# FFN weight combinations stored once in fp32 and split where they are used

## The chip, the cores and the metric

The kernel runs on one core of a Trainium2 chip. The metric is the device time of one execution in microseconds, as the median of several runs. The kernel before the change: 3426.71 us, median of 3 runs (3424.28 to 3429.13).

## What is computed

One transformer block for 2048 rows of width 576, with a modulation from a condition vector, 32 query heads over 16 key heads, a window of the last 512 keys, and a gated FFN of width 4608. Everything is float32.

```python
mod = (silu(c) @ w_mod).reshape(c.shape[0], 6, 1, -1)
sa, ca, ga, sb, cb, gb = (mod[:, i] for i in range(6))
h = layernorm(x) * (1 + ca) + sa
q = (h @ wq), 32 heads of 128
k, v = k_cache[:, :, -512:], v_cache[:, :, -512:], each for two query heads
p = softmax(q @ k.T * 128 ** -0.5)
x = x + ga * ((p @ v) @ wo)
h = layernorm(x) * (1 + cb) + sb
x = x + gb * ((sigmoid(h @ w_gate) * (h @ w_up)) @ w_down)
```

## The kernel before

**Arithmetic.** A float32 value is split into `hi`, its rounding to the type fp32r (a ScalarE copy with F32R as target), and `lo`, the rest (one subtraction). A product is three matmuls: hi x lo, lo x hi, hi x hi (`three`, line 272). Where weights are multiplied, the kernel uses a scheme with seven block products in place of eight: for w_gate/w_up, for w_down and for wo, sums and differences of blocks ("combinations") are formed first.

**Stage 1, attention** (loop at line 912). 128 blocks (a head and 512 queries), four steps each, so 512 steps `n`. A step does the scores of step n+2 (`scores`, `expo`), transposes the probabilities of step n (`transp`), does a quarter of the next-but-one query projection (`qproj`) and a quarter of the product with v of the block before (`pv`). ScalarE makes the exponentials `pp`, the hi copies `ptt` and `qt`; DVE the row maxima `neg`, the lo parts, and the scaled result `ov`. The reciprocal sums of a block go to DRAM and come back broadcast to all partitions (`put_rs`, `get_rs`, tile `rb`); `put_o` stores `ov` per block to `oscr`.

Beside the steps run **background jobs** (lines 675 to 831), listed by step in `at_step`. They read w_gate, w_up and w_down, form the combinations, split them in hi and lo, and store both to DRAM (`wsc`, `dsc`). There are 135 jobs, one each 3 steps: two per column tile of w_gate/w_up ("ab", one for each 128 rows), one per four tiles for the last 32 rows ("tail"), three per pair of row tiles of w_down ("down"). A job loads at step n, sums on GpSimd at n+3, makes hi on ScalarE at n+6 and lo on GpSimd at n+7, stores at n+8 and n+9. Its rooms lie in the tiles x0 and x1, whose contents are parked elsewhere by then, and in `extra`: three rooms for raw pieces, and two for `hi` (`(k % 2) * 7 * P` in line 708). 48 jobs for wo, one each 9 steps, form wo's combinations in tiles of their own and store them unsplit to `wosc`. All these instructions are pinned in program order with those around them (`pin`, `keep_order`); instructions that are not pinned may be moved by the scheduler.

**Stage 2, the product with wo** (line 1218). 32 visits (8 heads, 512 rows in four tiles) of seven products of 12 matmuls. `w_load` fetches a combination of wo, `w_split` splits it (ScalarE, and GpSimd or DVE), `v_load`, `v_sum` and `v_split` do the same for attention's result (tiles `vr`, `vt`, `vh`). DVE adds the products to x. In the last visits come the layer norm and the block sums for the FFN.

**Stage 3, the FFN** (line 1250). 72 rounds `u`: two pairs of row blocks by 36 column tiles. A round has seven products of seven matmuls of 512 columns (`product`, line 1112) with weights `sw`, loaded from `wsc` nine ahead (`load_w`), hi and lo in one DMA. Between them stand 42 matmuls of 288 columns with w_down (`down`, tile `sd`, `load_sd`, seven ahead), whose results DVE adds to the accumulators in x (`x<-w,x`; four banks `w`). ScalarE takes sums out of PSUM (`keep`), does sigmoids and hi copies (`hl`), GpSimd the lo parts and sums (`hl`, `vs`). Between the two pairs the input combinations are transposed anew (`load_combo`) and the results put together (`finish`).

In the profile nearly all rows are at L36, the helper that records instructions; tiles tell them apart. `x` is the background's rooms in stage 1, the residual in stage 2, the accumulators in stage 3.

Of the kernel before, what the change touches and what calls it, by code (L numbers as in the profile page):

```python
# [16 lines left out]
P = 128  # L17
# [27 lines left out]
def adaln_block_kernel(ctx: ExitStack, tc: tile.TileContext, x, k_cache, v_cache, wq, wo, w_gate, w_up, w_down,  # L45
# [251 lines left out]
    extra = at.tile([P, 4 * P], F32, tag="extra", name="extra")  # L297
# [187 lines left out]
    def expo(n):  # L485
        b, i = divmod(n, TPB)
        PP[n] = at.tile([P, W], F32, tag="pp", name="pp", bufs=2)
# [22 lines left out]
    def pv(b, k):  # L510
# [7 lines left out]
        if k == KT - 1:  # L518
            o = at.tile([P, BLK], F32, tag="ov", name="ov", bufs=2)
            by_tile = RB.pop(b).rearrange("p (q i) -> p i q", i=TPB)  # L520
            nc.vector.tensor_mul(o.rearrange("p (i q) -> p i q", i=TPB),
                                 OP_[b].rearrange("p (i q) -> p i q", i=TPB), by_tile)
            OT[b] = o
            del OP_[b], PT[b]
# [12 lines left out]
    def put_o(b):  # L537
        half, hd, blk = blk_of(b)
        to = oscr[half][hd // 8][:, :, 2 * (blk % 2) + hd % 2, hd // 2 % 4, :]
        keep_order(nc.sync.dma_start(to, OT.pop(b).rearrange("p (i q) -> p i q", i=TPB)))  # L540
# [138 lines left out]
    DW = D2 // 3  # L679
    jobs = []  # L680
    for f in range(NF):
        jobs += [("ab", f, 0), ("ab", f, 1)]
        if f % 4 == 3:
            jobs.append(("tail", f - 3, 0))
    jobs += [("down", g, s) for g in range(NF // 2) for s in range(3)]
# [14 lines left out]
    def bg_load(k, b0):  # L700
        kind, f, s = jobs[k]
        w = DW if kind == "down" else P
        raw = bg_view(b0, (k % 3) * 4 * P, [4, w])
        if k % 3 == 2:
            sums = extra[:, : 4 * w].rearrange("p (a b) -> p a b", a=4)
        else:
            sums = bg_view(b0 + 1, 14 * P, [4, w]) if k % 3 else bg_view(b0, 12 * P, [4, w])
        hi = bg_view(b0 + 1, (k % 2) * 7 * P, [8 if kind == "down" else 7, w])
        BG[k] = [raw, sums, hi]
        if kind == "down":  # L710
            for half, (i, j) in enumerate(((0, 1), (3, 2))):
                n0 = half * D2 + s * DW
                for c, slot in enumerate((i, j)):
                    r0 = (2 * f + c) * P
                    pin(nc.sync.dma_start(raw[:, slot, :], w_down[r0 : r0 + P, n0 : n0 + DW]))
            return
        if kind == "ab":
            r0, cc = s * P, slice(f * P, (f + 1) * P)
            g = w_gate[:, cc].rearrange("(c r) n -> r c n", c=2)[r0 : r0 + P]
            pin(nc.sync.dma_start(raw[:, 0:2, :], g))  # L720
            pin(nc.sync.dma_start(raw[:, 3, :], w_up[r0 : r0 + P, cc]))
            pin(nc.sync.dma_start(raw[:, 2, :], w_up[D2 + r0 : D2 + r0 + P, cc]))
            return
        for slot, w, r0 in ((0, w_gate, 2 * P), (1, w_gate, D2 + 2 * P), (3, w_up, 2 * P), (2, w_up, D2 + 2 * P)):
            src = w[r0 : r0 + TQ, f * P : (f + 4) * P].rearrange("r (q n) -> q r n", q=4)
            pin(nc.sync.dma_start(raw[:, slot, :], src))

    def bg_sums(k):
        r, m, hi = BG[k]
        kind, f, s = jobs[k]  # L730
        x0, x1, x2, x3 = [r[:, i, :] for i in range(4)]
        if kind == "down":
            for half in range(2):
                n0 = half * D2 + s * DW
                v = r[:, 2 * half : 2 * half + 2, :]
                g = rows2["gate"][:, None, n0 : n0 + DW].to_broadcast([P, 2, DW])
                pin(nc.gpsimd.tensor_mul(v, v, g))
            t1, t2, t3, t4 = [m[:, i, :] for i in range(4)]
            pin(nc.gpsimd.tensor_sub(t1, x3, x0))
            pin(nc.gpsimd.tensor_sub(t2, x2, t1))  # L740
            pin(nc.gpsimd.tensor_sub(t3, x2, x3))
            pin(nc.gpsimd.tensor_sub(t4, x1, t2))
            return
        s1, s2, s4, s3 = [m[:, i, :] for i in range(4)]
        pin(nc.gpsimd.tensor_add(s1, x3, x2))
        pin(nc.gpsimd.tensor_sub(s2, s1, x0))
        pin(nc.gpsimd.tensor_sub(s3, x0, x3))
        pin(nc.gpsimd.tensor_sub(s4, x1, s2))


    def bg_pairs(k):
        r, m, hi = BG[k]
        plain = [(7, 8, r[:, 3:4, :])] if jobs[k][0] == "down" and jobs[k][1] == NF // 2 - 1 else []
        return [(0, 3, r[:, 0:3, :]), (3, 7, m)] + plain

    def bg_hi(k):
        hi = BG[k][2]
        for a, b, v in bg_pairs(k):
            pin(nc.scalar.activation(hi[:, a:b, :].bitcast(F32R), v, AF.Copy))

    def bg_lo(k):
        hi = BG[k][2]
        for a, b, v in bg_pairs(k):
            pin(nc.gpsimd.tensor_sub(v.bitcast(F32R), v, hi[:, a:b, :]))

    def bg_store(k, part):
        kind, f, s = jobs[k]
        if part and kind != "tail":
            return
        hi = BG[k][2]  # L770
        if kind == "tail":
            for q in (0, 1) if part == 0 else (2, 3):
                rows = slice(q * TQ, (q + 1) * TQ)
                for to in range(4):
                    for a, b, src in bg_pairs(k) if to % 2 else [(0, 7, hi)]:
                        pin(nc.sync.dma_start(wsc[f + q][to * TQ : (to + 1) * TQ, a:b, 4, :], src[rows]))
        else:
            if kind == "down":
                to = [dsc[f][:, :, i, s * DW : (s + 1) * DW] for i in range(2)]
            else:  # L780
                to = [wsc[f][:, :, 2 * s + i, :] for i in range(2)]
            n = bg_pairs(k)[-1][1]
            pin(nc.sync.dma_start(to[0][:, :n], hi[:, :n]))
            for a, b, lo in bg_pairs(k):
                pin(nc.sync.dma_start(to[1][:, a:b, :], lo))
        if part or kind != "tail":
            del BG[k]

    STEP = 3
    slots = list(range(9, N - 50, STEP))[: len(jobs)]  # L790
    assert len(slots) == len(jobs)
# [8 lines left out]
    WOJ = {}  # L800

    def wo_load(k):
        g, c = divmod(k, 3)
        t = wp.tile([P, 7, DW], F32, tag="woj", name="woj", bufs=2)
        WOJ[k] = t
        for half, (i, j) in enumerate(((0, 1), (5, 2))):
            n0 = half * D2 + c * DW
            for h, slot in enumerate((i, j)):
                r0 = (2 * g + h) * P
                pin(nc.sync.dma_start(t[:, slot, :], wo[r0 : r0 + P, n0 : n0 + DW]))  # L810

    def wo_sums(k):
        t, c = WOJ[k], k % 3
        lo, hi = [rows2["gate1"][:, n0 : n0 + DW] for n0 in (c * DW, D2 + c * DW)]
        pin(nc.gpsimd.tensor_mul(t[:, 0:2, :], t[:, 0:2, :], lo[:, None, :].to_broadcast([P, 2, DW])))
        for slot in (2, 5):
            pin(nc.gpsimd.tensor_mul(t[:, slot, :], t[:, slot, :], hi))
        b11, b21, b22, t1, t2, b12, t4 = [t[:, i, :] for i in range(7)]
        pin(nc.gpsimd.tensor_sub(t1, b12, b11))
        pin(nc.gpsimd.tensor_sub(t2, b22, t1))  # L820
        pin(nc.gpsimd.tensor_sub(b12, b22, b12))
        pin(nc.gpsimd.tensor_sub(t4, b21, t2))

    def wo_store(k):
        g, c = divmod(k, 3)
        pin(nc.sync.dma_start(wosc[g // 4][:, :, g % 4, c * DW : (c + 1) * DW], WOJ.pop(k)))

    for k in range(3 * (H // 2)):
        at_n(32 + 9 * k, wo_load, k)
# [571 lines left out]
```

## Time and profile before

| | |
|---|---|
| median of the runs | 3426.71 us |
| the profiled execution | 3420.56 us |
| its span, first to last instruction | 3418.4 us |
| granted TensorE clock, mean | 0.962 |
| DMA packets; bytes | 721220; 623.08 MB |
| HBM read; written | 431.62 MB; 188.06 MB |
| weight loads in stage 3, sw and sd | 504 of 320 KB, 249 of 288 KB |

Attention ends near 1729 us of the span, the product with wo near 2164 us, the FFN with the span. In the rows of windows the columns are: stretch, its length, busy time of each engine with its count, granted clock, DMA share, GB/s. In rows of waits: who waited for whom, total us, times, longest. In rows of groups: operation, output and inputs with shapes, count, busy us, mean ns, idle time before it and what ended that.

### The profile page before, as it was taken

How to read it: one execution, taken by the hardware profiler on the slowest of the kernel's cores; microseconds unless marked ns; L12 is line 12 of the kernel's file. 1: busy time of each engine (PE TensorE's matmuls, PEld its weight loads, DVE VectorE, ACT ScalarE, POOL GpSimd, SP SyncE). 2: the span in 40 equal slices, each digit the busy share in tenths (PEclk: the TensorE clock that was granted, in tenths of full speed). 3: DMA queues.
4: the chain of work that ended last, by engine and by line, in shares of the span. 5: the costliest groups of instructions: out<-in, count | busy, mean ns of one | idle time of the engine just before them, and what ended most of it. 6: DMA issues, size and time to landing. Idle time of an engine off the chain costs nothing.

```text
span 3418.4 us, 50512 instructions
## 1 busy us (share of the span) xinstructions
PE 3111.2 (91%) x16629; PEld 2644.1 (77%) x16629; DVE 2085.1 (61%) x3621; ACT 1497.4 (44%) x3067; POOL 1746.9 (51%) x2124
## 2 busy tenths in 40 slices
PE   8987868887888998899979998999999999999999
PEld 6765656666667776778878897788888888888887
DVE  6555545554555555566678898665555575555557
ACT  5655544554555555555544443322322232222232
POOL 2655555654756666631076666355544354344443
PEclk9998889998999999999999999999999999999999
DMA  4788767777877777764343333766676677666664
GB/s 115 199 211 208 195 173 194 201 198 189 207 172 179 181 186 182 176 145 121 82 158 125 106 121 116 281 228 215 218 231 199 196 214 234 200 195 200 197 205 140
DMA packets 721220, 623.08 MB, mean 182 GB/s; under 512 B 255936, under 2 KB 584640, under 8 KB 715712
## 3 DMA queue, kind: packets, MB, share of 16 engines
q1 hardware_dynamic: 720352, 619.86, 64.9%
q8 instruction: 133, 2.18, 0.3%
q14 instruction: 127, 1.04, 0.1%
q10 hardware_dynamic: 608, 0.00, 0.0%
HBM read 431.62 MB, written 188.06 MB: 181 GB/s over the span
## 4 chain that ended last, share of the span: by engine, by line
PE 54%; DMA 18%; SPq 8%; POOL 7%; DVE 5%; issue 5%; ACT 3%; POOLq 0%; ACTq 0%; DVEq 0%
PE a L36 17%; PE w L36 12%; PE c L36 9%; SPq L36 8%; PE st L36 6%; DMA wsc<-x 5%; PE b L36 4%; PE qp L36 4%; DMA dsc<-x 4%; POOL x L36 3%; PE ot L36 3%; DMA x<-in_B_w_up_dram 2%; DMA x<-in_B_w_down_dram 2%; DVE vh L36 2%; DMA rb<-rscr 1%
## 5 line engine op out<-in xcount | busy, mean ns | idle before, releaser
L36 DVE TENSOR_TENSOR x<-w,x 128x288 f32<-128x288 f32 x980 | 442.8, 456 | 464.0 <-PE w L36 458.3
L36 PE MATMUL st<-kt,qt 128*128 128x512 f32 x1536 | 474.8, 414 | 129.9 <-ACT pp L36 125.6
L36 PE MATMUL a<-hc,sw 128*128 128x512 f32 x2016 | 583.5, 394 | 5.3 <-DVE v L36 3.8
L36 PEld LDWEIGHTS w<-sd,hl 128*128 128x128 f32 x3036 | 511.6, 188 | 90.3 <-DVE x L36 2.8
L36 PE MATMUL w<-sd,hl 128*128 128x288 f32 x3036 | 565.5, 296 | 3.0 <-POOL hl L36 1.1
L36 DVE TENSOR_REDUCE neg<-st 128x1 f32<-128x512 f32 x512 | 351.2, 687 | 307.4 <-PE st L36 306.0
L36 PE MATMUL qp<-hTm,wa 128*128 128x512 f32 x1536 | 457.5, 410 | 54.2 <-DVE qt L36 52.2
L36 PE MATMUL ot<-ptt,vs 128*128 128x512 f32 x1536 | 486.5, 429 | 12.1 <-DVE ptt L36 8.0
L36 DVE TENSOR_TENSOR ptt<-st,ptt 128x512 fp32r<-128x512 f32 x512 | 350.5, 686 | 216.2 <-ACT ptt L36 215.6
L36 PEld LDWEIGHTS st<-kt,qt 128*128 128x128 f32 x1536 | 294.4, 195 | 207.6 <-ACT pp L36 138.8
L36 ACT ACTIVATE ptt<-st 128x512 fp32r<-128x512 f32 x512 | 304.5, 595 | 292.3 <-PE st L36 291.4
L36 POOL TENSOR_TENSOR hl<-vs,hl 128x512 fp32r<-128x512 f32 x139 | 180.8, 1302 | 431.2 <-ACT hl L36 431.2
L36 PEld LDWEIGHTS a<-hc,sw 128*128 128x128 f32 x2016 | 355.9, 188 | 45.1 <-DVE v L36 4.9
L36 PEld LDWEIGHTS qp<-hTm,wa 128*128 128x128 f32 x1536 | 288.8, 194 | 131.4 <-DVE qt L36 66.8
L36 ACT ACTIVATE pp<-st,neg 128x512 f32<-128x512 f32 x512 | 351.4, 686 | 66.0 <-DVE neg L36 65.8
L36 PEld LDWEIGHTS st<-ident,pp 128*128 128x128 f32 x2048 | 262.7, 144 | 100.5 <-issue 21.7
L36 PE MATMUL st<-ident,pp 128*128 128x128 f32 x2048 | 318.9, 279 | 21.3 <-DVE rs L36 12.0
L36 PEld LDWEIGHTS ot<-ptt,vs 128*128 128x128 f32 x1536 | 266.9, 196 | 50.6 <-DVE ptt L36 13.0
L36 PE MATMUL c<-hc,sw 128*128 128x512 f32 x1008 | 303.9, 395 | 0.0
L36 POOL TENSOR_TENSOR x<-x,x 128x384 fp32r<-128x384 f32 (+6 forms) x313 | 252.3, 819 | 50.0 <-DVE x L36 23.5
L36 ACT ACTIVATE x<-x 128x384 fp32r<-128x384 f32 (+2 forms) x228 | 110.8, 522 | 293.4 <-DMA wsc<-x 158.6
L36 POOL TENSOR_TENSOR x<-x 128x128 f32<-128x128 f32 (+3 forms) x315 | 165.8, 540 | 84.6 <-DMA x<-in_B_w_up_dram 77.9
(176 smaller groups left out, 4663.0 us busy)
## 6 DMA issues: line engine op xcount, KB each, us to landing
sw<-wsc SPq DMA_DIRECT2D x504, 320.0 KB
sd<-dsc SPq DMA_DIRECT2D x249, 288.0 KB
rb<-rscr SPq DMA_DIRECT2D x128, 256.0 KB
oscr<-ov SPq DMA_DIRECT2D x128, 256.0 KB
vr<-oscr SPq DMA_DIRECT2D x32, 1024.0 KB
wsc<-x SPq DMA_DIRECT2D x72, 448.0 KB
dsc<-x SPq DMA_DIRECT2D x51, 336.0 KB
raw<-in_A_wq_dram SPq DMA_DIRECT2D x64, 256.0 KB
```

Source lines behind the costliest of these rows:

```text
L36: i = got(*args, **kw)
```

## The change

Eight edits:

1. `wsc` and `dsc` hold each FFN combination once, in fp32 (3 x 128 and 288 columns instead of 5 x 128 and 2 x 288). The FFN loads them raw (`sr`, four buffers; `dr`, three) and splits them itself: `split_w` with a ScalarE copy of 384 and a DVE subtraction of 256 elements into `sw` (five buffers instead of nine), `split_sd` with a ScalarE copy and a GpSimd subtraction of 288 into `sd` (six instead of seven).
2. The background has 79 jobs: 36 "ab" (a whole column tile), 9 "tail", 16 "wo", 18 "down". Only tails and wo are split.
3. A job takes one of four rooms, x0 to x3 (wo two of them), for 14 steps; jobs start 5 steps apart (wo at least 6). Rooms 2 and 3 are not given out from 50 steps before the middle to 4 after it. Loads at n, sums at n+4 and n+5, splits at n+6 and n+7, stores from n+8.
4. wo's combinations are split in attention and stored as hi and lo; `w_split` goes, and `w_load` fetches both into place, 1152 KB instead of 576, five of them ahead of stage 2.
5. `put_o` stores a head's two blocks together (64 DMAs with 1 KB rows instead of 128 with 512 B); `ov` has three buffers of twice the size, and `oscr`'s planes are in another order (`PLANE`).
6. `get_rs` is issued one step earlier.
7. x2 and x3 are loaded at steps 220 and 221 instead of 62 and 63; all four at 482 to 497, instead of x0 and x1 at 472 and 473.
8. `v_load` is two visits ahead with three buffers and issued at the first product of a visit instead of the fifth.

The core of the diff:

```diff
-wsc = [dram.tile([P, 7, 5, P], F32, tag=f"wsc{f}", name=f"wsc{f}") for f in range(NF)]
-dsc = [dram.tile([P, 8, 2, D2], F32, tag=f"dsc{g}", name=f"dsc{g}") for g in range(NF // 2)]
-wosc = [dram.tile([P, 7, 4, D2], F32, tag=f"wosc{q}", name=f"wosc{q}") for q in range(H // 8)]
+wsc = [dram.tile([P, 7, 3, P], F32, tag=f"wsc{f}", name=f"wsc{f}") for f in range(NF)]
+dsc = [dram.tile([P, 8, D2], F32, tag=f"dsc{g}", name=f"dsc{g}") for g in range(NF // 2)]
+wosc = [dram.tile([P, 7, 2, 4, D2], F32, tag=f"wosc{q}", name=f"wosc{q}") for q in range(H // 8)]
...
-    for k, n in enumerate(slots):
-        at_n(n, bg_load, k, 0)
-        at_n(n + 3, bg_sums, k)
-        at_n(n + 6, bg_hi, k)
-        at_n(n + 7, bg_lo, k)
-        at_n(n + 8, bg_store, k, 0)
-        at_n(n + 9, bg_store, k, 1)
+    for k, (kind, f) in enumerate(jobs):
+        need = 2 if kind == "wo" else 1
+        while True:
+            got = sorted((free[r], r) for r in range(NB) if free[r] <= n and
+                         n < N - 46 and not (r > 1 and n1 - 50 < n < n1 + 4))
+            if len(got) >= need:
+                break
+            n += 1
+            assert n < N
+        rooms = [r for _, r in got[:need]]
+        for r in rooms:
+            free[r] = n + 14
+        at_n(n, bg_load, k, rooms)
+        for part in range(2):
+            at_n(n + 4 + part, bg_sums, k, part)
+            if kind in ("wo", "tail"):
+                at_n(n + 6 + part, bg_split, k, part)
+        for part in range(4 if kind == "tail" else 1):
+            at_n(n + 8 + part, bg_store, k, part)
+        n += 6 if kind == "wo" else 5
...
+    def bg_split(k, part):
+        if jobs[k][0] == "tail":
+            r, m, hi = BG[k]
+            a, b, v = ((0, 3, r[:, 0:3]), (3, 7, m))[part]
+        else:
+            a, b = ((0, 4), (4, 7))[part]
+            v, hi = BG[k][0][:, a:b], BG[k][1]
+        pin(nc.scalar.activation(hi[:, a:b].bitcast(F32R), v, AF.Copy))
+        pin(nc.gpsimd.tensor_sub(v.bitcast(F32R), v, hi[:, a:b]))
...
+    def split_w():
+        if not SR:
+            return
+        u, a = next(iter(SR))
+        r = SR.pop((u, a))
+        t = fpool["h"].tile([P, 5, P], F32R, tag="sw", name="sw", bufs=5)
+        nc.scalar.activation(t[:, 0:3], r, AF.Copy)
+        nc.vector.tensor_sub(t[:, 3:5], r[:, 0:2], f32(t[:, 0:2]))
+        SW[u, a] = t
...
+    def split_sd():
+        if not DR:
+            return
+        g, a = next(iter(DR))
+        r = DR.pop((g, a))
+        t = fpool["p"].tile([P, 2, D2], F32R, tag="sd", name="sd", bufs=6)
+        nc.scalar.activation(t[:, 0], r, AF.Copy)
+        nc.gpsimd.tensor_sub(t[:, 1], r, f32(t[:, 0]))
+        SD[g, a] = t
...
-            at_late(n + 2, get_rs, b)
-            at_late(n + 6, put_o, b)
+            at_late(n + 1, get_rs, b)
+            if last_of[half * H + hd] == b:
+                at_late(n + 6, put_o, b)
...
     for b in range(2, NB):
-        at_n(60 + b, load_x, b)
-    for b in range(2):
-        at_n(N - 40 + b, load_x, b)
+        at_n(N // 2 - 38 + b, load_x, b)
+    for b in range(NB):
+        at_n(N - 30 + 5 * b, load_x, b)
```

How the instructions stand: ScalarE in attention, where the first background job's copies stood before (`x_101`, `x_102` are the tiles x0 and x1):

```order
L36 ACTIVATE pp,sum<-st,neg 128x512
L36 ACTIVATE x_102<-x_101 128x384
L36 ACTIVATE x_102<-x_101 128x512
L36 ACTIVATE ptt<-st 128x4x128
L36 ACTIVATE pp,sum<-st,neg 128x512
L36 ACTIVATE qt<-qp 128x512
```

and at the same place now:

```order
L36 ACTIVATE pp,sum<-st,neg 128x512
L36 ACTIVATE ptt<-st 128x4x128
L36 ACTIVATE pp,sum<-st,neg 128x512
L36 ACTIVATE qt<-qp 128x512
L36 ACTIVATE ptt<-st 128x4x128
```

The two copies of a background piece, and any wait in front of them, no longer stand between two steps. They do stand there in the jobs of wo, at about step 270; ScalarE now:

```order
L36 ACTIVATE pp,sum<-st,neg 128x512
L36 ACTIVATE x_102<-x_101 128x1152
L36 ACTIVATE ptt<-st 128x4x128
L36 ACTIVATE pp,sum<-st,neg 128x512
L36 ACTIVATE x_102<-x_101 128x864
L36 ACTIVATE qt<-qp 128x512
```

Each of these copies waits for GpSimd's sums of the same job. DVE in a round of the FFN, before (`x<-w,x` are the additions to the accumulators, `v` and `g` the FFN's own values):

```order
L36 TENSOR_TENSOR g_24974<-c,g_24974 128x512
L36 TENSOR_TENSOR x_103<-w,x_103 128x288 x2
L36 TENSOR_TENSOR v_24950<-a,v_24950 128x512
L36 TENSOR_TENSOR v_24950<-v_24950,g_24974 128x512
L36 TENSOR_TENSOR x_104<-w,x_104 128x288 x4
```

and the same part of a round now:

```order
L36 TENSOR_TENSOR g_23604<-c,g_23604 128x512
L36 TENSOR_TENSOR sw<-sr,sw 128x256
L36 TENSOR_TENSOR x_103<-w,x_103 128x288 x2
L36 TENSOR_TENSOR v_23574<-a,v_23574 128x512
L36 TENSOR_TENSOR sw<-sr,sw 128x256
L36 TENSOR_TENSOR v_23574<-v_23574,g_23604 128x512
L36 TENSOR_TENSOR x_104<-w,x_104 128x288 x3
```

A subtraction for a later product's weights stands about once per product among the additions that empty TensorE's banks.

More of the change, by code (lines that the diff above doesn't have):

```diff
@@ L751, in bg_pairs @@
     def bg_pairs(k):
         r, m, hi = BG[k]
[L753 to L764, printed above, removed]
+        return [(0, 3, r[:, 0:3, :]), (3, 7, m)]
@@ L770, in bg_store @@
-        hi = BG[k][2]
+        kind, f = jobs[k]
         if kind == "tail":
[L772 to L779, printed above, removed]
-            else:
[L781 to L785, printed above, removed]
@@ L812, in wo_sums @@
[L812 to L822, printed above, removed]
@@ L824, in wo_store @@
[L824 to L829, printed above, removed]
-        at_n(36 + 9 * k, wo_sums, k)
-        at_n(40 + 9 * k, wo_store, k)
+            hi = BG[k][2]
+            q = part
+            rows = slice(q * TQ, (q + 1) * TQ)
+            for to in range(4):
+                for a, b, src in bg_pairs(k) if to % 2 else [(0, 7, hi)]:
+                    pin(nc.sync.dma_start(wsc[f + q][to * TQ : (to + 1) * TQ, a:b, 2, :], src[rows]))
+        elif part == 0:
+            if kind == "ab":
+                pin(nc.sync.dma_start(wsc[f][:, :, 0:2], BG[k][:, 0:7]))
+            elif kind == "down":
+                n = 8 if f == NF // 2 - 1 else 7
+                pin(nc.sync.dma_start(dsc[f][:, :n], BG[k][0][:, :n]))
+            else:
+                for i in range(2):
+                    pin(nc.sync.dma_start(wosc[f // 4][:, :, i, f % 4], BG[k][1 - i][:, :7]))
```

224 lines of the change are left out of this document (103 added, 121 removed).

## The prediction

> **What bounds the kernel now.** I read the page first: engines' shares, then the slices of the span.
>
> ```profile
> PE 3111.2 (91%) x16629; PEld 2644.1 (77%) x16629; DVE 2085.1 (61%) x3621; ACT 1497.4 (44%) x3067; POOL 1746.9 (51%) x2124
> PE   8987868887888998899979998999999999999999
> PEclk9998889998999999999999999999999999999999
> ```
>
> TensorE is the busiest, but a busy share mixes three stages. Attention fills slices 1 to 20 (to about 1729 us), the product with `wo` the next five (to 2164), the FFN the rest. Only attention shows eights and sevens, and a granted clock below 9. So the second view is the windows of the row-maximum (`neg`, one per step of 128 queries, 512 in all): the count on DVE says how many steps each stretch held.
>
> ```profile
> 65.00:800.00 735.00, 138.54 (x202) 156.86 (x404) 0.90 0.76 193
> 800.00:950.00 150.00, 30.77 (x45) 34.14 (x88) 0.93 0.78 204
> 950.00:1300.00 350.00, 75.42 (x111) 85.48 (x220) 0.95 0.75 179
> 1300.00:1500.00 200.00, 44.33 (x65) 50.53 (x130) 0.99 0.76 178
> 1500.00:1700.00 200.00, 51.25 (x75) 57.99 (x150) 1.00 0.38 96
> ```
>
> The last stretch, where the background jobs are nearly over, runs at 200 / 75 = 2.67 us a step. The others run at 3.64, 3.33, 3.15 and 3.08. At 2.67 they would have taken 539, 120, 296 and 173 us instead of 735, 150, 350 and 200: the background costs attention 196 + 30 + 54 + 27 = 307 us. Third view, the waits of TensorE between 65 and 1700 us:
>
> ```profile
> PE st L36 <- ACT pp L36: 132.8, 36, 16.4
> PE qp L36 <- DVE qt L36: 50.3, 23, 13.0
> PE st L36 <- DVE rs L36: 12.0, 1, 12.0
> ```
>
> These 195 us are idle TensorE, and two thirds of it waits for ScalarE's exponentials. What ScalarE itself waited for in that time:
>
> ```profile
> ACT x L36 <- DMA wsc<-x: 158.6, 27, 16.7
> ACT x L36 <- DMA dsc<-x: 46.5, 21, 5.4
> ACT wa L36 <- DMA raw<-in_A_wq_dram: 45.6, 24, 5.2
> ACT x L36 <- POOL x L36: 31.3, 20, 4.3
> ACT wm L36 <- DMA wm<-in_w_mod_dram: 27.1, 3, 11.5
> ACT x L36 <- DMA dsc<-extra: 12.5, 3, 4.5
> ```
>
> One event in the timeline shows the mechanism, first ScalarE, then TensorE:
>
> ```profile
> 773.49 0.20 ACT L36 ACTIVATION_READ_ACCUMULATOR pp<-st,neg 128x1 f32 x1
> 790.43 1.04 ACT L36 ACTIVATE x<-x 128x384 fp32r<-128x384 f32 x2 [16.73 <-DMA wsc<-x]
> 792.68 0.80 PE L36 MATMUL st<-kt,qt 128*128 128x512 f32 x1 [16.39 <-ACT pp L36]
> ```
>
> ScalarE stands in order. The `hi` copy of a background piece may not overwrite its room before the store of the piece two jobs earlier has landed; the exponential behind it waits 16.7 us, and TensorE stands still for 16.4.
>
> **Part A, attention.** Pieces of w_gate, w_up and w_down lose their `hi` copies (117 + 54 + 54 + 27 + 18 + 3 copies in before, by the order; 50 remain, 18 for the tails and 32 for `wo`), and a room now lives 14 steps, with its store issued at the eighth. So the waits of ScalarE on wsc, dsc and on POOL's x go. They are 158.6 + 46.5 + 31.3 + 12.5 = 249 us against 73 us for the rows that stay (wa, wm); by that share, 0.77 of TensorE's 183 us behind pp and qt, 141 us, go. The 12.0 us behind `rs` go too: there DVE waited once, 21.1 us, at four layer-norm rows of block 2 that a load at step 62 had let forward to step 121; the load is now at step 220.
>
> ```profile
> DVE h L36 <- POOL wm L36: 21.1, 1, 21.1
> ```
>
> Idle TensorE explains 195 of the 307 us. The rest, 112, goes with the clock: 735 x 0.10 + 150 x 0.07 + 350 x 0.05 + 200 x 0.01 = 104 us of full rate were not granted, some of it while TensorE stood anyway. With three quarters of the stalls gone I take half of the 104 back, 52 (ends 0 and 104). By the Trainium skill (TensorE: Matmul & The Clock Gate, Part 1) the clock falls to half after an idle window of about 3.4 us and returns after a busy one; the rows agree so far that 0.90 stands where the 16 us waits are and 1.00 where none is. By that rule alone the clock would come back wholly with the long stalls, and the sum would be some 25 us lower.
>
> Against that come new stalls. 16 jobs of `wo` put copies of 1152 and 864 elements on ScalarE, behind GpSimd's sums, which wait for loads; nine tails keep theirs. At the mean wait of the POOL row above, 31.3 / 20 = 1.6 us, 25 jobs x 2 copies would be 80 us of ScalarE, of which, as now, some 0.57 reaches TensorE (183 of 322 us): 46. Their POOL work lies well apart in the order, so I take 30 (ends 0 and 100). **A = -141 - 12 - 52 + 30 = -175 us**, ends -90 and -280.
>
> At nothing: GpSimd's background work falls (no `lo` of the FFN weights) and lies beside TensorE as now. SP issues 2164 DMAs instead of 2913, nearly all of the 749 from attention. `get_rs` passes one step's loads on SP and needs only the 2 KB store ahead of it; `put_o` stores a pair of blocks at once, later, and is read only in the next stage; the reload of x at steps 220 and 482 to 497 has eight steps ahead of its first reader. If SP's queue were full, these would cost; it is emptier than before.
>
> **Part B, the product with wo.** Windows, and the groups of 1729 to 2098 us:
>
> ```profile
> 1729.00:2098.00 369.00, 336.80 (x2407) 329.51 (x2408) 215.29 (x199) 126.45 (x200) 0.98 0.37 128
> 1957.00:2030.00 73.00, 69.50 (x512) 68.20 (x511) 64.66 (x88) 31.37 (x48) 42.79 (x26) 1.00 0.32 111
> ```
> ```profile
> L36 POOL TENSOR_TENSOR wc<-wr,wc 128x1152 fp32r<-128x1152 f32 x9 | 27.6, 3065 | 1.7 <-ACT wc L36 1.7
> L36 POOL TENSOR_TENSOR wb<-wr,wb 128x1152 fp32r<-128x1152 f32 x6 | 18.2, 3042 | 2.5 <-ACT wb L36 2.5
> L36 DVE TENSOR_TENSOR vh<-vr,vh 128x512 fp32r<-128x512 f32 x114 | 136.9, 1200 | 10.1 <-ACT vh L36 10.0
> ```
>
> The splits of `wo` go. Where few of them ran (1957 to 2030) a matmul costs 73 / 512 = 0.143 us; over the whole stretch 369 / 2407 = 0.153. At 0.143 the stretch takes 344 us: -25. The 28 loads double from 576 to 1152 KB, with a DMA share of 0.37 to lie in; three or four of them at each quarter's end have one visit of some 11 us to land. I put 3 us on that. The last 60 us, full of layer norm, stay. **B = -22 us**, ends -45 and +10.
>
> **Part C, the FFN.** Here the stored halves are made anew at each use: 504 times a ScalarE copy of 384 and a DVE subtraction of 256 elements, 249 times a ScalarE copy and a GpSimd subtraction of 288.
>
> ```profile
> 2285.00:2420.00 135.00, 135.00 (x729) 118.09 (x728) 77.83 (x156) 39.55 (x68) 72.19 (x59) 1.00 0.64 198
> 2758.00:2782.00 24.00, 24.00 (x160) 21.70 (x159) 19.63 (x35) 13.36 (x26) 9.49 (x16) 1.00 0.84 269
> 2800.00:2817.00 17.00, 17.00 (x94) 14.88 (x93) 15.71 (x32) 4.10 (x7) 12.13 (x13) 1.00 0.66 190
> 3362.00:3387.00 25.00, 23.93 (x141) 20.93 (x139) 22.88 (x46) 5.99 (x11) 18.45 (x18) 1.00 0.53 149
> ```
> ```profile
> L36 ACT ACTIVATE x<-x 128x384 fp32r<-128x384 f32 x117 | 60.7, 519 | 171.6 <-DMA wsc<-x 146.0 <-POOL x L36 12.9 <-POOL extra L36 4.5
> L36 ACT ACTIVATE x<-x 128x288 fp32r<-128x288 f32 x54 | 24.0, 444 | 116.2 <-DMA dsc<-x 46.5 <-POOL x L36 12.9 <-DMA wsc<-x 12.6
> L36 POOL TENSOR_TENSOR x<-x,x 128x288 fp32r<-128x288 f32 x54 | 43.5, 806 | 0.5
> L36 DVE TENSOR_TENSOR x<-x,x 128x288 f32<-128x288 f32 x32 | 23.4, 735 | 0.4
> L36 DVE TENSOR_TENSOR v<-v,g 128x512 f32<-128x512 f32 x25 | 18.0, 718 | 2.6
> ```
>
> The first row is TensorE without a gap: 135 us hold 729 matmuls, eight of the 72 rounds of 49 + 42, so 16.88 us a round, and fewer bytes can save nothing there. Per round DVE is busy 9.7 us, ScalarE 4.9, GpSimd 9.0. The change adds seven splits of weights and 3.5 of down: ScalarE 7 x 0.52 + 3.5 x 0.44 = 5.2, GpSimd 3.5 x 0.81 = 2.8, DVE 7 times d. For 256 elements from SBUF the nearest row is 0.735 for 288, which gives d = 0.65; the ends are 0.36 (half of 0.718) and 1.2 (the vh row, twice as long and beside a busy GpSimd). With 0.65 DVE is busy 14.3 of 16.88 us. Raw pieces are loaded four ahead and split four products ahead of use, so a steady round stays at 16.88. Where DVE has no such room it is late: at the change of pairs (19.63 + 4.6 of 24, 15.71 + 4.6 of 17) about 4 us, at the end (22.88 of 25, fewer splits left) 3, at the start, where a copy and a subtraction now stand between the first load and the first matmul, 1, and 4 us for single rounds. **C = +12 us**, ends -5 and +90 (72 x (9.7 + 8.4 - 16.88) at d = 1.2).
>
> **Sum.** The profiled execution took 3420.6 us, 2.2 more than its span; 3420.6 - 175 - 22 + 12 = 3235.6. The median of the runs is 6 us above that execution, so I say 3240 for a median.
>
> **The rivals.**
> *DVE becomes the bound in the FFN.* In-order DVE would hold back the sums that empty TensorE's banks. Price 72 x (9.7 + 7d - 16.88). At d = 1.2 it is 90 us instead of 12, total about 3320. It ends **slower than before** only if it eats the 197 us of A and B: d above 1.41 us for 256 elements. Against that: no DVE row of that length comes near; for it: the vh row is 1200 ns where v<-v,g of the same shape is 718. The Trainium skill (SBUF — State Buffer, SBUF: two separate sides) says that a DVE operation with two SBUF inputs and a GpSimd operation that reads SBUF exclude each other for a whole instruction; the two rows agree with it, and it speaks against this change, which puts 504 such subtractions beside GpSimd. By that rule each waits for at most one GpSimd instruction, 1.3 us at most, on top of its own time.
> *Attention's wait only moves.* ScalarE would wait for GpSimd, and that for loads, in the `wo` phase above all; A falls to some -75: 3340. For it is the row below, GpSimd waiting for loads that had three steps' lead; against it: the lead is four steps now and SP's queue shorter.
>
> ```profile
> POOL extra L36 <- DMA x<-in_B_w_up_dram: 210.1, 23, 18.6
> ```
>
> *The background becomes free*: all four stretches near 2.67 us a step, -280 in A and -35 in B: about 3112 with C at 0.
> That the change doesn't do what it says is out: the order shows the copies gone.
>
> **How the numbers follow.** Forecast 3190 to 3295: 0.66. DVE bound but still faster: 0.07; DVE bound and slower: 0.05; the wait moves: 0.12; free background: 0.10. Two tenths may be left out: I leave out the free background and the slower case and reach from 3140 to 3355, which takes in A's worse end (about 3325) and the two cases at 3320 and 3340. A measurement of this kernel tells 0.2% from no change; faster by more than that 0.94, within it 0.01, slower 0.05.
>
> **What would show it.** Right: below 2.9 us a step between 65 and 1200 us, no ScalarE wait on wsc or dsc, granted clock above 0.95 there, attention's end near 1540; the wo stretch near 0.143 us a matmul; FFN rounds of 16.88 us with DVE near 85%. Wrong: ScalarE rows x<-x waiting for POOL by the ten microseconds; TensorE in the FFN waiting for DVE's x; a subtraction of 256 elements above 1 us.

## The result and the profile after

The changed kernel takes **3146.04 us** (median of 4 runs, 3144.07 to 3152.01), the kernel before 3425.49 in the same series (3420.56 to 3429.13). The ratio is 0.9188 (95% interval 0.9171 to 0.9205): 8.1% faster. That is inside the range, 6 us above its lower end of 3140, but 94 us below the predicted 3240 and below the forecast's own 3190 to 3295. The profiled execution took 3147.1 us, its span is 3145.3. One slow execution of the last kernel below, at 6526.5 us, is left out of its figures.

The gain of the span, 3418.4 - 3145.3 = 273.1 us, divides so, by instants of the two traces (last row maximum `neg`, first product with wo, first FFN product):

| part | before | after | change | forecast |
|---|---|---|---|---|
| to the last `neg` | 1712.2 | 1430.7 | -281.6 | -175 |
| from there to the first wo product | 16.5 | 19.7 | +3.2 | 0 |
| the product with wo | 435.7 | 395.3 | -40.5 | -22 |
| the FFN | 1253.9 | 1299.7 | +45.7 | +12 |

The page of the changed kernel, engines and slices:

```profile
PE 3048.5 (97%) x16629; PEld 2619.5 (83%) x16629; DVE 2288.3 (73%) x4116; ACT 1721.0 (55%) x3569; POOL 1655.2 (53%) x1531
PE   8999999999999999998999889999999989999998
PEclk9999999999999999999999899999999999999999
```

TensorE executes as many matmuls as before in 62.7 us less busy time, and 97% of the span is busy. The kernel moves 503.86 MB in 435570 packets, where the one before moves 623.08 MB in 721220. The eights that are left mark the ends of stages and, in slice 33, the change of pairs. The windows of `neg` in attention of the changed kernel (columns as before):

```profile
65.00:800.00 735.00, 181.60 (x264) 205.10 (x530) 0.99 0.72 187
800.00:1420.00 620.00, 159.88 (x232) 179.43 (x464) 1.00 0.65 191
```

735 / 264 = 2.78 and 620 / 232 = 2.67 us a step: beside 2.67, the background costs some 30 us in the first stretch and nothing in the second. TensorE's waits between 65 and 1420 us, and behind them ScalarE's:

```profile
PE st L36 <- ACT pp L36: 4.2, 4, 3.6
PE st L36 <- DVE rs L36: 2.8, 1, 2.8
```
```profile
ACT ptt L36 <- PE st L36: 430.1, 453, 5.7
...
ACT wa L36 <- DMA raw<-in_A_wq_dram: 4.8, 2, 2.5
ACT wm L36 <- DMA wm<-in_w_mod_dram: 3.6, 1, 3.6
```

Of TensorE's idle 195 us in three rows, 7 us are left in two. No row of ScalarE with x is among them, and the loads `wa` and `wm`, which the prediction kept as "rows that stay", fell from 72.7 to 8.4 us as well. ScalarE now mostly waits for TensorE. Windows of the product with wo (first row), of rounds of the FFN with a late layer norm, of the change of pairs, and of the second pair's steady rounds:

```profile
1450.00:1766.00 316.00, 315.50 (x2353) 315.23 (x2354) 270.94 (x412) 123.51 (x195) 170.29 (x109) 0.99 0.50 183
1922.00:1965.00 43.00, 36.98 (x187) 31.39 (x186) 30.15 (x58) 19.18 (x40) 32.41 (x29) 0.96 0.42 129
2450.00:2574.00 124.00, 114.65 (x631) 99.39 (x630) 102.67 (x194) 65.88 (x135) 81.97 (x82) 0.97 0.49 150
2590.00:3067.00 477.00, 477.00 (x2553) 416.93 (x2552) 353.24 (x731) 261.29 (x532) 290.29 (x252) 1.00 0.40 113
```

In wo a matmul costs 316 / 2353 = 0.134 us. In the steady FFN TensorE has no gap, with DVE busy 353.24 / 477 = 74%, not the 85% forecast; but 477 / 2553 = 0.1868 us a matmul, 17.0 us a round of 91, stands against 135 / 729 = 0.1852, 16.85. In the second and third row TensorE stands for 6.0 and 9.4 us. The groups of the new subtractions, on DVE and on GpSimd:

```profile
L36 DVE TENSOR_TENSOR sw<-sr,sw 128x256 fp32r<-128x256 f32 x504 | 289.8, 576 | 101.9 <-ACT sw L36 75.1
L36 POOL TENSOR_TENSOR sd<-dr,sd 128x288 fp32r<-128x288 f32 x249 | 217.2, 874 | 181.3 <-ACT sd L36 181.3
```

The subtraction on DVE, the prediction's d, takes 0.576 us on average, below the 0.65 assumed; single ones run from 0.37 to 1.66. The one on GpSimd takes 0.874 where 0.81 was taken. A rule of the Trainium skill stood behind the rival here (SBUF — State Buffer, SBUF: two separate sides: a DVE operation with two SBUF inputs and a GpSimd operation that reads SBUF exclude each other). The trace agrees with it: the 183 subtractions that start while GpSimd executes nothing take 0.418 us on average and never more than 0.427; the 321 that start during a GpSimd instruction take 0.666 on average, and nine of ten of them end 0.279 to 0.286 us after that instruction ends, however long it had still to run. So they stand until it is over; the longest loses 1.24 us, within the 1.3 of the prediction. Over all 504 subtractions the mean wait is 0.16 us, a small price.

**Where the FFN lost.** DVE's, ScalarE's and TensorE's waits in the FFN, three views of the changed kernel:

```profile
DVE x L36 <- PE w L36: 196.0, 348, 1.2
DVE sw L36 <- ACT sw L36: 75.1, 56, 4.8
```
```profile
ACT sw L36 <- DMA sr<-wsc: 41.4, 14, 5.3
```
```profile
PE w L36 <- DVE x L36: 14.5, 11, 2.8
PE a L36 <- DVE v L36: 13.9, 8, 4.8
PE w L36 <- DMA x<-scr: 5.1, 1, 5.1
```

One event in the timeline of the changed kernel, with SP, ScalarE, DVE and TensorE in turn:

```profile
1941.72 2.31 SPq L36 DMA_DIRECT2D scr<-h  x2
1944.12 0.38 SPq L36 DMA_DIRECT2D sr<-wsc  x1
1946.62 0.52 ACT L36 ACTIVATE sw<-sr 128x384 fp32r<-128x384 f32 x1 [5.34 <-DMA sr<-wsc]
1947.17 0.42 DVE L36 TENSOR_TENSOR sw<-sr,sw 128x256 fp32r<-128x256 f32 x1 [4.80 <-ACT sw L36]
1948.11 1.18 DVE L36 TENSOR_TENSOR x<-w,x 128x288 f32<-128x288 f32 x3
1948.62 1.09 PE L36 MATMUL w<-sd,hl 128*128 128x288 f32 x3 [2.81 <-DVE x L36]
```

SP stands behind a store of `h`, the late layer norm's result, so the raw weights behind it come late. ScalarE's copy waits 5.34 us for them, DVE's subtraction 4.80 for the copy, and the sums `x` that empty TensorE's banks stand behind the subtraction. In the kernel before, a nine-deep buffer was filled by the DMA alone, and TensorE waited 1.1 us for DVE's `x` in the whole FFN; now it is 14.5. The weights that are late are now in front of instructions that TensorE waits for.

By rounds the 45.7 us are: rounds 0 to 2 59.1 from 52.7 us (+6.4; the 5.1 us row is there); rounds 4, 5, 14, 15 with a late layer norm 82.8 from 67.5 (+15.3); rounds 9, 19, 20 some +3.4; the change of pairs, rounds 34 to 39, 124.0 from 114.8 (+9.2); the last two 48.2 from 43.8 (+4.4); the remaining 54 rounds 0.13 each (+7.0).

### The profile page after: what moved, and what is told of

Same layout as the page of the kernel before. It is cut to its first block, busy times and chain, and to the rows that moved or that the text cites. A ratio compares the mean times of both kernels' runs of the same rounds, so it can differ in the third digit from the quotient of the medians.

```text
span 3145.3 us, 49956 instructions
## 1 busy us (share of the span) xinstructions
PE 3048.5 (97%) x16629; PEld 2619.5 (83%) x16629; DVE 2288.3 (73%) x4116; ACT 1721.0 (55%) x3569; POOL 1655.2 (53%) x1531
## 2 busy tenths in 40 slices
DMA packets 435570, 503.86 MB, mean 160 GB/s; under 512 B 51184, under 2 KB 392816, under 8 KB 426096
## 4 chain that ended last, share of the span: by engine, by line
PE 87%; DVE 5%; POOL 3%; DMA 3%; issue 2%; ACT 1%; SPq 1%; ACTq 0%; DVEq 0%; POOLq 0%
PE a L36 19%; PE st L36 18%; PE qp L36 13%; PE w L36 12%; PE ot L36 11%; PE c L36 10%; PE b L36 5%; DVE x L36 2%; POOL x L36 1%; DMA rscr<-rs 1%; DMA sr<-wsc 1%; SPq L36 1%; DVE sw L36 1%; POOL h L36 0%; DVE v L36 0%
## 5 line engine op out<-in xcount | busy, mean ns | idle before, releaser
L36 PE MATMUL w<-sd,hl 128*128 128x288 f32 x3036 | 574.5, 299 | 15.5 <-DVE x L36 14.5
L36 DVE TENSOR_TENSOR x<-w,x 128x288 f32<-128x288 f32 x980 | 429.3, 452 | 197.2 <-PE w L36 192.2
L36 PE MATMUL st<-kt,qt 128*128 128x512 f32 x1536 | 447.0, 398 | 4.0 <-ACT pp L36 4.0
L36 PE MATMUL qp<-hTm,wa 128*128 128x512 f32 x1536 | 446.9, 400 | 3.9 <-DVE qt L36 2.1
L36 ACT ACTIVATE pp<-st,neg 128x512 f32<-128x512 f32 x512 | 350.3, 684 | 48.2 <-DVE neg L36 47.7
L36 DVE TENSOR_TENSOR sw<-sr,sw 128x256 fp32r<-128x256 f32 x504 | 289.8, 576 | 101.9 <-ACT sw L36 75.1
L36 ACT ACTIVATE sw<-sr 128x384 fp32r<-128x384 f32 x504 | 259.0, 515 | 153.6 <-issue 83.3
L36 POOL TENSOR_TENSOR x<-x 128x256 f32<-128x256 f32 (+3 forms) x334 | 246.7, 758 | 153.6 <-DMA x<-in_B_w_up_dram 101.1
L36 PE MATMUL st<-ident,pp 128*128 128x128 f32 x2048 | 308.8, 274 | 5.3 <-DVE rs L36 2.8
L36 POOL TENSOR_TENSOR sd<-dr,sd 128x288 fp32r<-128x288 f32 x249 | 217.2, 874 | 181.3 <-ACT sd L36 181.3
L36 PEld LDWEIGHTS ot<-ptt,vs 128*128 128x128 f32 x1536 | 253.6, 191 | 28.1 <-DVE ptt L36 3.1
```

Source lines behind the costliest of these rows:

```text
L36: i = got(*args, **kw)
```

## The experiments

The kernels are compared by the instant of the last `neg` and by stages, from their profiled executions; all but the last variant ran once. In kernels whose FFN is that of the changed one, the FFN took 1295.3 to 1301.4 us, so 6 us in that stage say nothing. Dots in a diff stand for lines left out, most of which follow from those shown.

**The loads of x2 and x3 later, in the kernel before.**

```diff
-        at_n(60 + b, load_x, b)
+        at_n(N // 2 - 38 + b, load_x, b)
```

> The kernel before, with x2 and x3 loaded at steps 220 and 221 instead of 62 and 63, nothing else. Theory (the layer-norm rows of block 2 stood too early on DVE): TensorE's 12 us wait behind rs near step 121 goes, the last row maximum comes 10 to 20 us earlier than 1712 us. Rival (the wait belongs to the modulation's late loads and shows wherever the layer norm stands): it comes back near step 233, and the last row maximum stays within 5 us of 1712.

3423.5 us beside 3427.95; last `neg` at 1708.2 instead of 1712.2. Neither expectation holds whole: DVE's 21 us wait does not come back near step 233, but TensorE's waits for `pp` rise from 132.8 to 143.1 us, and the end of attention moves by 4 us, not 12. Executions of the kernel before differ by 9 us among themselves.

**Six rooms for hi instead of two, in the kernel before,** with the edit above. Rooms of the tiles x1 to x3 are used, so that ScalarE finds a free one; so all four tiles are loaded again at steps 482 to 497, as in the changed kernel.

```diff
-        hi = bg_view(b0 + 1, (k % 2) * 7 * P, [8 if kind == "down" else 7, w])
+        rb, ro = hi_room(k)
+        hi = bg_view(rb, ro, [8 if kind == "down" else 7, w])
...
+        return 1 + k % 6 // 2, (k % 2) * 7 * P
```

> As b_load_x, and the hi copies of the 135 background jobs go to six rooms (two each in x1, x2, x3) instead of two, except in the 49 steps around the middle; every copy, sum, split and store of before is still made. Theory (ScalarE waits for the store that still reads its room): ScalarE's waits for wsc and dsc fall from 218 us to below 40, the last row maximum comes at 1500 to 1570 us instead of 1712. Rival (the copies' own time, the lo parts on GpSimd, or the DMA traffic set the pace): the waits change their name, the last row maximum stays above 1640.

3411.0 us; last `neg` at 1699.1. Only 13 us of 282. ScalarE's waits of this kernel between 65 and 1700 us:

```profile
ACT wa L36 <- DMA raw<-in_A_wq_dram: 118.5, 35, 17.0
ACT x L36 <- POOL x L36: 75.6, 54, 5.3
ACT x L36 <- DMA x<-in_B_w_up_dram: 56.5, 16, 11.0
ACT x L36 <- DMA wsc<-x: 32.7, 6, 14.4
```

Against 158.6 us for wsc<-x before, the room's wait is down to 32.7, but wq's loads rose from 45.6 to 118.5 and those of w_up are new. **The theory of the prediction falls:** ScalarE's wait for a room was what it met first among things that were late, and without it the next late one holds it for nearly as long.

**Without the stores, in the kernel before.** All loads, sums, copies and subtractions stay; what isn't stored is read from the first combination in the FFN.

```diff
+        if f:
+            if part or kind != "tail":
+                del BG[k]
+            return
...
-            d = nc.sync.dma_start(f32(t), wsc[u % NF][:, a])
+            d = nc.sync.dma_start(f32(t), wsc[0][:, a])
```

> The kernel before, leaving out the background's stores of FFN combinations for all column tiles and row pairs but the first, which the FFN then reads for all of them (so the FFN computes with wrong weights); loads, sums, copies and splits on ScalarE and GpSimd are all still made. Wider rooms for hi alone (b_hi_rooms) gave 9 us in attention. Theory (the stores' traffic makes every transfer late, and in-order ScalarE hands that on wherever it waits): without it the last row maximum comes at 1460 to 1530 instead of 1712. Rival (the background's own work on ScalarE and GpSimd): above 1620.

3159.4 us; last `neg` at 1451.2, -261 us of the change's -282, with an FFN as before (1252 us). The windows of `neg`:

```profile
65.00:800.00 735.00, 177.45 (x259) 199.51 (x516) 0.99 0.54 139
800.00:1200.00 400.00, 102.93 (x150) 115.82 (x300) 1.00 0.52 127
```

2.84 and 2.67 us a step with every ScalarE copy and GpSimd subtraction of the kernel before. So the stores held attention up, not the work of splitting. On the chip of this run the kernel before took 3396.9 us, 29 less than beside the changed kernel, and there is no profile of it from there; up to some 29 of the 261 us may be the chip's.

**The other way round, three kernels from the changed one.** First ScalarE copies of "ab" and "down" pieces in place, at the steps where the hi copies were:

```diff
+            else:
+                at_n(n + 6 + part, bg_copy, k, part)
```

> The kernel after, with a ScalarE copy of every ab and down piece onto itself at n+6 and n+7 (54 jobs, 7 blocks each), so that ScalarE has the background work of before again, behind the same sums, but no wait for a store's room. Theory (the wait, not the work): the last row maximum stays within 15 us of 1431. Rival (work on ScalarE): some 110 us of copies, of which 0.57 reaches TensorE: above 1480.

3158.4 us; last `neg` at 1443.9, +13. The background's copies on ScalarE add up to 150.0 us there, to 43.8 in the changed kernel and 144.9 in the one before: the copies alone cost little. Then every "ab" and "down" piece is stored a second time, to a place that nothing reads:

```diff
+                pin(nc.sync.dma_start(wsx[f], BG[k][:, 0:7]))
...
+                pin(nc.sync.dma_start(dsx[f][:, :n], BG[k][0][:, :n]))
```

> The kernel after, with each ab and down store issued a second time into DRAM that nothing reads: 54 stores and 50 MB more, which brings the bytes written in attention back to about those of before. Theory (rooms live long enough that a late landing holds up nobody): the last row maximum within 10 us of 1431. Rival (DMA traffic was a cause by itself): above 1470.

3178.3 us; last `neg` at 1460.2, +29.5. Its windows:

```profile
65.00:800.00 735.00, 174.66 (x255) 196.81 (x508) 0.98 0.79 224
800.00:1430.00 630.00, 161.80 (x236) 181.69 (x470) 1.00 0.73 226
```

The 29.5 us lie between the two expectations: traffic costs something. But this is more traffic per time than before (193 and 204 GB/s in the first stretches), with the DMA engines as busy (0.79 and 0.73 where it was 0.76), at 2.88 and 2.67 us a step. So bytes by themselves do not bring the old time back. Then the number of DMAs, seven or eight per store (325 more), and the size of rows, 512 B where the changed kernel has 1 KB:

```diff
-                pin(nc.sync.dma_start(wsc[f][:, :, 0:2], BG[k][:, 0:7]))
+                for i in range(7):
+                    pin(nc.sync.dma_start(wsc[f][:, i, 0:2], BG[k][:, i]))
...
```

> The kernel after, with every ab and down store issued as seven or eight DMAs, one for each combination: same bytes, for ab the same 1 KB rows, 325 more issues on SP. Theory (SP's in-order issue was full before, 0.73 to 0.77 of its time against 0.57 to 0.61 after in the ab phase, and that made loads late): the last row maximum comes at 1450 to 1480. Rival (packets or bytes): within 8 us of 1431.

```diff
-                pin(nc.sync.dma_start(wsc[f][:, :, 0:2], BG[k][:, 0:7]))
+                pin(nc.sync.dma_start(wsc[f][:, :, 0:3:2], BG[k][:, 0:7]))
...
```

> The kernel after, with the two row blocks of a gate or up combination kept apart in wsc, so that the ab stores write 512 B rows instead of 1 KB, with the same bytes and as many DMAs. In a_stores 50 MB more in 54 DMAs cost attention 29 us. Theory (the DMA engines are paid by packet): the 32000 packets that are added here cost about as much in the ab phase, the last row maximum comes at 1445 to 1465 instead of 1431. Rival (bytes or issues count): within 5 us of 1431.

3142.4 and 3142.1 us; last `neg` at 1431.2 and 1431.4. Neither costs anything, and the theory of both expectations missed. The second adds some 32000 packets, a seventh of the 226000 by which the two kernels differ between 65 and 1420 us, so it speaks for the size of these rows alone.

**What tells the long attentions from the short.** SP's own waits between 65 and 1420 us, in the kernel before, with six rooms for hi, without the stores, in the changed kernel and with its stores doubled:

```profile
SPq L36 <- DMA wsc<-x: 108.1, 64, 4.6
SPq L36 <- POOL x L36: 89.7, 130, 2.6
SPq L36 <- DMA dsc<-x: 70.0, 38, 3.9
SPq L36 <- DVE rs L36: 25.0, 8, 12.2
```
```profile
SPq L36 <- DMA wsc<-x: 99.1, 60, 4.8
...
SPq L36 <- DMA dsc<-x: 71.4, 35, 4.3
SPq L36 <- DVE rs L36: 14.6, 8, 4.5
```
```profile
SPq L36 <- DVE rs L36: 256.9, 102, 6.6
```
```profile
SPq L36 <- DVE rs L36: 289.7, 78, 9.6
```
```profile
SPq L36 <- DVE rs L36: 191.5, 62, 9.7
```

`rs` is the foreground's own. An SP that waits long for it has issued all that came before and is ahead; an SP that hardly waits for it is behind. In the two kernels with a long attention it waits for `rs` 15 to 25 us, in the others, with the one of 325 more DMAs (235.9), 190 to 290. In the two long ones its issuing, summed over its timeline, fills 74 and 75% of the 1355 us, and the landing of earlier FFN stores another 170 to 178 us, nearly all of it before loads of w_gate and w_down: job k's raw pieces take the room of job k-3, whose store is issued only one step earlier. With the waits for POOL's x that is 94% of the time: by these rows **SP's queue was full**, and what stood in it late. In the short ones issuing fills 48 to 57%.

Issuing alone is not the cause. Between 65 and 400 us SP issues for 240 us both in the kernel before and in the one with 325 more DMAs; yet a step takes 335 / 95 = 3.53 us in the first and 335 / 121 = 2.77 us in the second:

```profile
65.00:400.00 335.00, 64.55 (x95) 72.83 (x188) 0.91 0.76 195
```
```profile
65.00:400.00 335.00, 83.20 (x121) 93.64 (x242) 1.00 0.72 197
```

What only the long attentions have beside the issuing is SP's wait for the background's stores to land: 174 us and more between 65 and 1420 us, at most 15 in the short ones. The prediction's own event fits: ScalarE's 16.7 us to 790.43 lie in a row of 24 tail stores, with four loads between them, that SP issues in the kernel before; these are its first and its last row:

```profile
771.53 1.29 SPq L36 DMA_DIRECT2D wsc<-x  x2
...
789.23 0.43 SPq L36 DMA_DIRECT2D wsc<-extra  x1
```

This last step is read from traces, not shown by a run of its own: to leave the stores out takes away bytes, issues and room waits at once. The kernel before with longer-lived rooms for raw pieces alone wasn't run.

**The FFN.** First six raw buffers `sr` instead of four:

```diff
-            t = fpool["h"].tile([P, 3, P], F32, tag="sr", name="sr", bufs=4)
+            t = fpool["h"].tile([P, 3, P], F32, tag="sr", name="sr", bufs=6)
...
```

> The kernel after, with six raw weight buffers sr instead of four in the FFN. Theory (in rounds 4, 5, 14 and 15 ScalarE stands before a raw piece that SP issued late, behind the stores of the second pair's layer norm): two more products of lead, 4.8 us, cover most of the waits of up to 5.3 us; these four rounds fall from 82.7 us to about 72, the span by 8 to 12 us. Rival (DVE has too much to do in these rounds): they stay above 80 us.

3138.9 us; rounds 4, 5, 14, 15 take 74.5 us instead of 82.8, but round 20 23.0 instead of 18.4; the FFN 1290.6, -9 and 3 us below the shortest with four buffers. Part of the chain goes, part moves. Second, the stores of `h` on GpSimd's queue, so that SP doesn't stand behind them:

```diff
-            nc.sync.dma_start(d[:, c : c + v.shape[1], :], v)
+            nc.gpsimd.dma_start(d[:, c : c + v.shape[1], :], v)
```

> The kernel after, with the stores of late_tile issued from GpSimd's queue, behind the sums that they store, instead of SP's. Theory (SP waits in order for GpSimd's sums and holds up the loads of weights behind them): the waits of SP for h and tt, 41 us, and ScalarE's for sr in rounds 4, 5, 14, 15 go; the span falls by 10 to 18 us. Rival (DVE's load): no change beyond 4 us.

3148.5 us; the four rounds 88.3, worse. ScalarE's waits for `sr` fall from 34.7 to 6.0 us between 1850 and 2250, and in their place it has this row:

```profile
ACT hl L36 <- POOL vs L36: 21.1, 16, 5.9
```

GpSimd is late instead, and what ScalarE has to copy for DVE stands behind a `hl` that waits for GpSimd. As these rows read, the chain from ScalarE over DVE to TensorE's banks stays and starts at another engine; no run takes the chain away. Third, the block order of `sw` as before, against the 0.13 us of a steady round:

```diff
-        nc.scalar.activation(t[:, 0:3], r, AF.Copy)
-        nc.vector.tensor_sub(t[:, 3:5], r[:, 0:2], f32(t[:, 0:2]))
+        nc.scalar.activation(t[:, 0:5:2], r, AF.Copy)
+        nc.vector.tensor_sub(t[:, 1:4:2], r[:, 0:2], f32(t[:, 0:3:2]))
...
```

> The kernel after, with the five blocks of sw in the order of before (hi, lo, hi, lo, hi) instead of hi, hi, hi, lo, lo. A steady round takes 17.01 us where it took 16.88. Theory (the place of the weights in their tile): a round falls back to 16.9 us, the span by about 8 us. Rival (the extra semaphores, or the other buffers' addresses): a round stays at 17.0 us.

3146.0 us, a steady round 17.0: not the layout.

**The start of wo.** In the changed kernel the last `rs` but one is stored at 1424.70 and its `rb` fetched at 1441.81, behind 5.9 MB of wo's weights; only then are the last `rs` stored (1442.22) and its `rb` fetched (1445.14), and TensorE stands 12.85 us:

```profile
1424.70 0.32 SPq L36 DMA_DIRECT2D rscr<-rs  x1
1441.81 0.32 SPq L36 DMA_DIRECT2D rb<-rscr  x1
```
```profile
1450.38 3.01 PE L36 MATMUL a<-wb,vh 128*128 128x288 f32 x11 [12.85 <-DVE ov L36]
```

With four of the five weight loads, and a `vr`, put later:

```diff
-            for s in range(5):
-                w_load(0, s)
+            w_load(0, 0)
+        if k in (7, 8, 9, 10):
+            w_load(0, k - 6)
...
```

> The kernel after, with only the first combination of wo loaded at step 505, the next four at steps 512 to 515 and the second visit's vr at 516, behind the last broadcast of the reciprocal sums. Theory (5.9 MB of weights stand on the DMA engines before the last rscr and rb, and TensorE waits 12.9 us for ov): that wait falls to about 7 us, the first product with wo starts 5 to 8 us earlier. Rival (the wait is the round trip of the last rb itself): it stays above 11 us, or the first visits lose what is gained.

3148.2 us. The wait falls to 4.88 us and the first product starts at 1440.4, but the first two visits take 22.9 and 13.6 us instead of 12.7 and 11.6: the weights are late there. The wait only moved.

**Three edits together:** six raw buffers, the subtraction one product later than its copy, and three of the five first weights loaded later.

```diff
...
+        if LOS:
+            t, r = LOS.pop()
+            nc.vector.tensor_sub(t[:, 3:5], r[:, 0:2], f32(t[:, 0:2]))
...
-        nc.vector.tensor_sub(t[:, 3:5], r[:, 0:2], f32(t[:, 0:2]))
+        LOS.append((t, r))
```

> The kernel after, with three edits: six raw buffers sr instead of four; DVE's subtraction for sw issued one product after ScalarE's copy; the third to fifth combinations of wo and the second vr loaded at step 512 instead of 505. Theory (DVE's in-order queue waits behind the subtraction for a late ScalarE copy, and TensorE's banks for DVE): DVE's 75 us of waits for ScalarE's sw fall below 25, rounds 4, 5, 14, 15 from 82.8 to about 72 us, the start of the wo stage comes 4 to 8 us earlier; 3125 to 3138 us. Rival (DVE and GpSimd simply have too much to do in those rounds): they stay above 80 us, 3138 to 3147.

3134.0 us in the profiled run (3126.1 to 3135.1 over five), ratio to the kernel before 0.922 (0.9204 to 0.9236). This is the chip on which the kernel before took 3396.9, and the changed kernel was not run there; the two variants of it that were and cost nothing in attention took 3142. So it beats the changed kernel by some 8 to 12 us, an estimate, as executions of the changed kernel differ by 8 us. DVE's waits for ScalarE's `sw` fall from 75.1 to 52.4 us only, where below 25 was expected; rounds 4, 5, 14, 15 take 74.3 us. The FFN takes 1289.6, hardly less than with the six buffers alone; the later subtraction shows no gain that could be told. The first product with wo starts 11.5 us behind the last `neg` instead of 19.7, but the stage behind it takes 401.5 us instead of 395.3.

## Why the prediction was right and wrong

- **The direction and the place were right.** Attention paid for the background by waits at ScalarE, and they went, and the step time fell: 2.78 and 2.67 us where "below 2.9" was asked; the clock stands at 0.99. Attention's end came at 1450 us, not "near 1540".
- **That the range held owes something to luck.** It left out the rival that came true in A and B, and reached down to 3140; C's loss, nearly four times the forecast, brought the time back to 3146. The 6 us by which a median was to lie above the profiled execution did not show either: the changed kernel's median lies 1 us below its own.
- **The mechanism of part A was wrong.** "The `hi` copy of a background piece may not overwrite its room before the store of the piece two jobs earlier has landed" is what the row says, and with six rooms 13 us came, not 141. The stores made everything late (-261 us without them), by the traces through a full SP queue in which loads wait for stores to land; that last step has no run of its own. "At nothing ... If SP's queue were full, these would cost; it is emptier than before" looked at the changed kernel only and did not ask whether the queue was full before. That would also be why the rows `wa` and `wm`, which the share of 0.77 kept, went too.
- **Part A's sizes.** Stalls: -188 us (195 to 7) where -141 - 12 + 30 = -123 was said. The new stalls of 30 us did not come: no row of ScalarE's `x` is left. GpSimd's late loads were the stores' doing too; without the stores its row `extra` falls from 210.1 to 4.7 us. Clock: 104 us were missing before, now 735 x 0.01 = 7; -97 where half, -52, was taken. Together they are 285; 281.6 was measured. The rule quoted from the Trainium skill (TensorE: Matmul & The Clock Gate, Part 1) had the clock come back wholly with the long stalls, and the trace agrees: 0.99 and 1.00, up from 0.90 in the first stretch, with one wait of 3.6 us left. The prediction priced that at "some 25 us"; all of the 104 in place of half is 52.
- **A misreading of the page.** "Only attention shows eights and sevens" is wrong: slices 21 (a seven) and 25 (an eight) lie, all but the first's beginning, in the product with wo. No term of the sum hangs on it.
- **The 12 us at step 121** were no gain by themselves (4 us): in a stage whose loads are late elsewhere, one wait less is made up by the next.
- **Part B** was right in kind, -40.5 for -22. The term of 0.143 us a matmul was mis-sized: its stretch still held 88 DVE and 48 ScalarE instructions, and TensorE was busy in it 69.50 of 73 us. Without splits it is 0.134, and the 3 us for the quarters' ends did not show. Not in the sum was the wait at the stage's start, +3.2.
- **Part C** failed in "a steady round stays at 16.88 ... about 4 us" at the change of pairs "and 4 us for single rounds". The subtraction was cheaper than assumed, so DVE as the bound was no danger; but the cost was counted as DVE's load, and it came as a chain of in-order engines wherever raw weights or GpSimd are late: +15.3 in four rounds, +9.2 at the pairs' change, +6.4 at the start for 1, +4.4 at the end for 3, +3.4 in three other rounds. The 54 quiet rounds gave +7 for 0. Two of the three signs of being wrong are there: TensorE waits for DVE's `x` (14.5 us), and 23 of the 504 subtractions take more than 1 us.
- **The rivals.** DVE as the bound is out: TensorE has no gap in 477 us with DVE at 74%. "The wait only moves" did not happen in attention. "The background becomes free" is what happened, with its -280 in A and -35 in B; its 3112 had C at 0, and with C's 46 us it is 3158, 12 above the measured 3146. It was given 0.10.

## What to carry to other kernels

The name in a wait's row is only what an in-order engine met first among late things; before a cause is made of it, look at the queue that issues the transfers, and ask whether that queue waits for the foreground (ahead) or hardly ever (behind). A wait for a buffer to be stored can cost most where it stands in the queue that all loads share. Here, as the traces read, rooms that live longer and fewer stores were worth more than the engine work saved: 106 us of ScalarE copies put back cost 13 us. When a DMA that fills an operand directly is replaced by a load and two in-order instructions, count the rounds in which the load is late, not the busy time of a steady one.

## What the runs showed of the hardware

The same bytes in little more than half the packets take only a tenth less of the DMA engines' time. The DMA view between 65 and 1420 us, of the kernel before and of the changed one (packets, MB, share of 16 engines):

```profile
q1 hardware_dynamic: 512928, 255.34, 75.6%
```
```profile
q1 hardware_dynamic: 286432, 255.05, 68.3%
```

And a steady round without any gap got 0.13 us longer. By the distances of starts, in rounds 42 to 67 of both kernels, the 288-column matmuls take 134.6 ns where they took 132.4 (42 a round, 0.09 us), those of 512 columns 231.8 where they took 231.1 (49 a round, 0.04 us). The clock was granted in full in both; the cause stays open.
